# Block-sparse attention with a gated MLP behind it: small tiles gathered in front, large tiles at round SBUF addresses, the sampled words loaded as one plain row

## The chip, the core and the metric

The kernel runs on one core of one Trainium2 chip. Times are device microseconds (us) of one execution. The core has TensorE (PE, with its weight loads shown apart as PEld), VectorE (DVE), ScalarE (ACT), GpSimd (POOL) and SyncE (SP). SP, ACT and POOL issue DMAs; sixteen DMA engines carry them out. SBUF has 128 partitions, and a tile's address below is the byte at which it starts in each of them.

## What is computed

```python
# batch 4, heads 8, sequence 768, head size 64, blocks of 32, 3 sampled blocks per query block
scores = scale * np.matmul(q, k.transpose(0, 1, 3, 2))
...
mask = mask | (blk_i == 0) | (blk_j == 0) | (blk_i == n_blocks - 1) | (blk_j == n_blocks - 1)
for qb in range(n_blocks):
    for kb in sampled_blocks[qb]:
        mask[qb * block:(qb + 1) * block, kb * block:(kb + 1) * block] = True
...
x = attn_out.transpose(0, 2, 1, 3).reshape(B * S, H * D)      # 3072 x 512
h = x @ w_in                                                 # 512 x 2048
g = h * (1.0 / (1.0 + np.exp(-1.702 * h)))
return (g @ w_out).astype(np.float32)                        # 2048 x 512
```

The mask also holds each block's own neighbours. `sampled_blocks` is int64, 24 x 3 values.

## The kernel before

The 3072 tokens are worked in `NC` = 6 chunks of `CT` = 512. Each chunk needs eight units of attention (64 query rows of all heads each), which fill one chunk tile pair `xhi`, `xlo`; there are `NX` = 3 such pairs, `x[0]`, `x[1]`, `x[2]`, used in turn. Every fp32 factor of the MLP is held as a high and a low half in fp32r, and every product is three matmuls: high by high, high by low, low by high.

`first` (line 903) works the attention of the first chunk while inputs still arrive. `tick` (line 694) then runs 64 steps, one for each pair of a chunk (the first four) and one of the 16 slices of 128 hidden columns. A step has `up` (line 548), 12 matmuls in the order L557, L558, L559 with a slice of `win` as weights (the stationary operand) and 512 columns of `xhi` or `xlo` streamed through (the moving operand); the gate on ACT and DVE into `ghi` and `glo`; and `down` (line 588) for the step before, 12 matmuls at L608, L609 and L604 with `ghi` or `glo` as weights and 512 columns of `wout` streamed. Attention of later chunks is put between the steps by `plan`. `last` and `pair` (lines 890 and 835) do the last two chunks together, in seven products of half size for eight: L817 in `half`, with `win`, or sums of them in `shi`, `slo`, as weights and `x` or `t2hi`, `t2lo` streamed. In all there are 768 matmuls at L557 to L559, 1152 at L604 to L609 and 336 at L817, each of 128x128 weights and 512 columns.

`win0` to `win6` and `wout0` to `wout2` lie in the pool `const`; `win7` to `win15` in the pool `late`, which takes the room of the opening tiles once those are done with; `x[2]` in the pool `stage`, behind `late`. `ghi`, `glo`, `g` and `wst` lie in the pool `work`. `prepare` closes the attention pools and opens `tail` at the right end. No address is written in the code: pools are stacked in the order in which they are opened, those of the left from below, those with `side="right"` from the top, so a small tile in one pool shifts all that come behind it.

`run` (line 959) sets the order of the opening. SP issues, in this order: the keys of batch 0 (`kres`, three DMAs at L220), the sampled words for value loads (`sbr`, L140), the same words in all partitions (`scratch`, L153), values (`vown`, L250), queries (`qt`, L206), the keys of batch 1 (L220, two DMAs), and so on. L140 takes the low half of each int64:

```python
        self.sbr = const.tile([1, NB, NR], I32, name="sbr")
        nc.sync.dma_start(out=self.sbr.rearrange("p a b -> p (a b)"), in_=sb32.rearrange("(o a c) -> o a c", o=1, c=2)[:, :, 0])
```

`load_k` (line 210) reads single words of `sbr` into registers, on POOL at L233 and on SP at L243.

Of the kernel before, what the change touches and what calls it, by code (L numbers as in the profile page):

```python
# [9 lines left out]
F32 = mybir.dt.float32  # L10
F32R = mybir.dt.float32r
I32 = mybir.dt.int32
# [6 lines left out]
P = 128  # L19
B, H, S, D = 4, 8, 768, 64  # L20
BLK = 32
NB = S // BLK
NPAIR = H // 2
NR = 3
# [30 lines left out]
class Kernel:  # L55
# [4 lines left out]
    def __init__(self, ctx, tc, q, qd, kb, kT, v, vd, sb, w_in, w_out, out):  # L60
        self.tc, self.nc = tc, tc.nc
        self.q, self.qd, self.kb, self.kT, self.v, self.vd, self.sb = q, qd, kb, kT, v, vd, sb
        self.w64, self.out = (w_in.bitcast(I32), w_out.bitcast(I32)), out
        self.ctx = ctx
        pool = self.pool = lambda name, bufs, **k: ctx.enter_context(tc.tile_pool(name=name, bufs=bufs, **k))
        self.const = pool("const", 1)
        self.work = pool("work", 2)
        self.attnpool, self.wordpool = ExitStack(), ExitStack()
        self.attn = self.attnpool.enter_context(tc.tile_pool(name="attn", bufs=1, side="right"))
        self.words = self.wordpool.enter_context(tc.tile_pool(name="words", bufs=3, side="right"))  # L70
        self.small = pool("small", 6)
        psum = pool("psum", 1, space=PSUM)
        dram = pool("dram", 1, space=DRAM)
        self.ws = [dram.tile([P, DM], F32, name=f"ws{f}") for f in range(NF)]
        self.banks = psum.tile([P, 8, 512], F32, name="banks")
        self.bank = [self.banks[:, i] for i in range(8)]
        c = self.const


        self.kg = [self.attn.tile([P, 12, 2, NPAIR * BLK], F32, name=f"kg{i}") for i in range(RING)]  # L80
        self.qt = [self.attn.tile([P, 2, NPAIR * UT], F32, name=f"qt{i}") for i in range(RING)]
        self.opening = ExitStack()
        early = self.opening.enter_context(tc.tile_pool(name="opening", bufs=1))
        vpool = [self.attn] * RING + [early]
        self.vown = [p.tile([P, 2, 2 * VROW], F32, name=f"vown{i}") for i, p in enumerate(vpool)]
        self.vmid = [p.tile([P, 2 * VROW], F32, name=f"vmid{i}") for i, p in enumerate(vpool)]
        self.win = [c.tile([P, 2 * DM], F32R, name=f"win{f}") for f in range(NWIN)]
        self.wout = [c.tile([P, 2 * DM], F32R, name=f"wout{i}") for i in range(WRING)]
        self.x = [(c.tile([P, NCT, CT], F32R, name=f"xhi{i}"), c.tile([P, NCT, CT], F32R, name=f"xlo{i}"))
                  for i in range(2)]  # L90
        self.kres = early.tile([P, 2, NPAIR, S], F32, name="kres")
        self.raw4 = early.tile([P, 2 * DM], I32, name="raw4")
        self.pts = [self.attn.tile([P, 4, P], F32, name=f"pt{i}") for i in range(3)]
        self.pts += [self.work.tile([P, 4, P], F32, name=f"pt{3 + i}", tag=("ghi", "glo")[i % 2]) for i in range(3)]
        self.npt = 0
        self.kmidof, self.vmidof = [None] * RING, [None] * (RING + 1)
        self.units, self.kent, self.vent, self.items = [], [], [], []

        def entry(of, **more):
            of.append({"n": len(of), "scores": 0, "values": 0, **more})  # L100
            return of[-1]

        def item(k, v, **more):
            k["scores"] += 1
            v["values"] += 1
            self.items.append({"n": len(self.items), "unit": self.units[-1], "k": k, "v": v, **more})

        def dense(b):
            entry(self.units, b=b, u=None)
            k = entry(self.kent, b=b, u=None)  # L110
            for i in range(2):
                v = entry(self.vent, b=b, u=None, i=i)
                item(k, v, i=i, first=i == 0, end=i == 1)

        def sparse(b0, u):
            k, v = (entry(of, b=b0, u=u) for of in (self.kent, self.vent))
            for b in (b0, b0 + 1):
                entry(self.units, b=b, u=u)
                item(k, v, first=True, end=True)

        for b in range(2):
            dense(b)
        sparse(0, 0)
        for b in range(2, B):
            dense(b)
        for n in range(1, 2 * NU):
            sparse(n // NU * 2, n % NU)
        for n, e in enumerate(self.vent):
            e["at"] = n % (RING + 1) if n < NV3 else (n - NV3) % RING
            e["behind"] = next((o for o in reversed(self.vent[:n]) if o["at"] == e["at"]), None)  # L130
        self.knext = self.vnext = 0
        self.early = True
# [3 lines left out]
    def indices(self):  # L136
        nc, const = self.nc, self.const
        sb32 = self.sb.bitcast(I32).rearrange("a b -> (a b)")
        self.sbr = const.tile([1, NB, NR], I32, name="sbr")
        nc.sync.dma_start(out=self.sbr.rearrange("p a b -> p (a b)"), in_=sb32.rearrange("(o a c) -> o a c", o=1, c=2)[:, :, 0])  # L140
        scratch = self.work.tile([P, CT], F32, name="scratch", tag="g")
        at = [0]

        def take(shape):
            n = 1
            for k in shape:
                n *= k
            flat = scratch[:, at[0]:at[0] + n]
            at[0] += n
            return flat.rearrange("p (a b) -> p a b", a=shape[0]) if len(shape) == 2 else flat  # L150
# [16 lines left out]
                           allow_small_or_imprecise_dtypes=True)  # L167
        qb = take([NB])
        nc.gpsimd.iota(qb, pattern=[[1, NB]], base=0, channel_multiplier=0, allow_small_or_imprecise_dtypes=True)
        self.ident = const.tile([P, P], F32, name="ident")  # L170
        make_identity(nc, self.ident)
        yield
        nc.vector.memset(vblk[:, 0:NB:NB - 1], 0.0)
# [18 lines left out]
        for i in range(NR):  # L192
            for cols, rows in ((first, slice(BLK * i, BLK * (i + 1))), (second, slice(BLK * (i + 1), BLK * (i + 2)))):
                nc.vector.tensor_copy(out=vblk[rows, cols], in_=rr[rows, cols, i])
        self.vidx = const.tile([P, 2, NB], I32, name="vidx")
        vrow = take([NB])
        nc.vector.tensor_scalar(out=vrow, in0=vblk, scalar1=float(BLK), scalar2=lane, op0=ALU.mult, op1=ALU.add)
        for b in range(2):
# [87 lines left out]
            pass  # L286

    def psum(self, what, k):  # L290

        early, late = {"s": ((0, 1), (2, 3)), "t": ((4, 5), (4, 5)), "a": ((6,), (7,))}[what], {"s": (0, 1), "t": (0, 1), "a": (2,)}[what]
        return early[k % 2] if self.early else late
# [754 lines left out]
```

## Time and profile before

| | |
|---|---|
| median of 3 runs (lowest to highest) | 753.39 us (751.44 to 754.46) |
| the profiled execution's own time | 752.94 us |
| its span, first to last instruction | 751.2 us |
| PE busy | 726.3 us, 97% of the span |
| DVE, ACT, POOL busy | 450.5, 388.5, 64.9 us |
| chain that ended last | PE 74%, DVE 10%, DMA 9%, ACT 4% |
| DMA | 122.97 MB, mean 164 GB/s |

How to read it: the ends of matmuls are modelled, and a matmul of 512 columns is shown some 395 ns long while the next one starts some 230 ns after it. So "busy" on PE says only that no gap is wider than about 0.16 us, and the pace of PE is read from the starts of successive matmuls, not from their durations.

### The profile page before, as it was taken

The page shows a single profiled execution, that of the slowest core. Times are in us where ns is not written, and L with a number is a line of the kernel's source. Part 1 is how long each engine was busy: PE and PEld are TensorE (multiplying, and loading weights), DVE is VectorE, ACT ScalarE, POOL GpSimd, SP SyncE. Part 2 cuts the span into 40 slices and gives each one's busy share as a digit, 9 for nine tenths or more (in the row PEclk, how much of TensorE's full clock was granted, in tenths as well). Part 3 has the DMA queues.
Part 4 walks back from the last instruction along what each step waited for, and adds up shares of the span by engine and source line. Part 5 has one row for each costly group of instructions (what it writes and reads, how often), then busy time and mean ns, then how long its engine had stood idle before and what let it go on. Part 6 is the DMA issues. An engine that isn't in the chain of part 4 may idle for free.

```text
span 751.2 us, 18756 instructions
## 1 busy us (share of the span) xinstructions
PE 726.3 (97%) x7564; PEld 562.8 (75%) x7564; DVE 450.5 (60%) x839; ACT 388.5 (52%) x759; POOL 64.9 (9%) x105
## 2 busy tenths in 40 slices
PE   7988999998999999999999999999999999999996
PEld 4656777676777777777877777777777788888885
DVE  4676788789654444455444534544576877676542
ACT  4676666666554454445444444544334554545442
POOL 1336201011000110100000000100000000000000
PEclk9999999999999999999999999999999999999999
DMA  8988877768476576657565555630111311110532
GB/s 305 353 319 273 263 263 249 243 213 283 169 230 184 154 207 194 178 159 235 171 186 174 168 167 173 198 98 30 43 43 42 85 28 43 29 42 29 145 107 70
DMA packets 58858, 122.97 MB, mean 164 GB/s; under 512 B 7188, under 2 KB 24980, under 8 KB 58772
## 3 DMA queue, kind: packets, MB, share of 16 engines
q1 hardware_dynamic: 45060, 76.72, 33.8%
q0 software_dynamic: 6336, 23.43, 9.4%
q10 hardware_dynamic: 7376, 21.63, 8.5%
q8 instruction: 59, 0.97, 0.5%
q14 instruction: 27, 0.22, 0.1%
HBM read 111.26 MB, written 10.49 MB: 162 GB/s over the span
## 4 chain that ended last, share of the span: by engine, by line
PE 74%; DVE 10%; DMA 9%; ACT 4%; issue 2%; SPq 1%; ACTq 0%; DVEq 0%
PE banks L604 10%; PE banks L608 10%; PE banks L609 10%; PE banks L817 9%; PE banks L557 6%; PE banks L558 6%; PE banks L559 6%; PE banks L393 5%; PE banks L364 5%; PE banks L315 5%; DMA raw<-in_moe_w_in_dram 2%; DMA vmid<-in_v_dram 2%; DMA raw<-in_moe_w_out_dram 2%; DVE a L509 1%; PE banks L325 1%
## 5 line engine op out<-in xcount | busy, mean ns | idle before, releaser
L609 PE MATMUL banks<-wout,ghi 128*128 128x512 f32 x384 | 152.0, 396 | 1.7 <-DVE wout L477 1.7
L608 PE MATMUL banks<-wout,ghi 128*128 128x512 f32 x384 | 153.2, 399 | 0.0
L604 PE MATMUL banks<-wout,glo 128*128 128x512 f32 x384 | 109.6, 399 | 0.6 <-DVE glo L585 0.6
L346 ACT ACTIVATE ex<-banks,nm 128x256 f32<-128x256 f32 x176 | 69.2, 479 | 77.4 <-DVE rg L409 77.4
L557 PE MATMUL banks<-xhi,win 128*128 128x512 f32 x256 | 105.5, 412 | 1.1 <-DVE g L572 0.8
L559 PE MATMUL banks<-xhi,win 128*128 128x512 f32 x256 | 100.9, 394 | 0.0
L558 PE MATMUL banks<-xlo,win 128*128 128x512 f32 x256 | 100.9, 394 | 0.0
L546 DVE TENSOR_TENSOR wout<-wst,wout 128x512 fp32r<-128x512 f32 x80 | 55.2, 691 | 68.6 <-ACT wout L545 66.2
L609 PEld LDWEIGHTS banks<-wout,ghi 128*128 128x128 f32 x384 | 72.1, 188 | 19.1 <-DVE wout L477 2.5
L608 PEld LDWEIGHTS banks<-wout,ghi 128*128 128x128 f32 x384 | 72.0, 188 | 17.6 <-ACT ghi L577 0.3
L604 PEld LDWEIGHTS banks<-wout,glo 128*128 128x128 f32 x384 | 70.7, 188 | 18.9 <-DVE glo L585 2.2
L565 ACT ACTIVATE g<-banks 128x512 f32<-128x512 f32 x64 | 38.6, 603 | 87.9 <-PE banks L559 87.9
L370 ACT COPY pt<-banks 128x512 f32<-128x512 f32 x112 | 60.9, 589 | 32.4 <-PE banks L364 29.0
L261 POOL DMA_INDIRECT vown<-in_v_dram,vidx x44 | 44.2, 1004 | 381.3 <-PE banks L393 370.1
L577 ACT CAST ghi<-g 128x512 fp32r<-128x512 f32 x80 | 50.1, 626 | 44.2 <-DVE g L572 38.0
L572 DVE SCALAR_TENSOR_TENSOR g<-g,banks 128x512 f32<-128x512 f32 x51 | 35.0, 686 | 60.4 <-ACT g L565 60.1
L332 DVE TENSOR_REDUCE mx<-banks 128x4 f32<-128x1024 f32 x44 | 53.7, 1221 | 25.6 <-PE banks L315 25.6
L364 PEld LDWEIGHTS banks<-ident,ex 128*128 128x128 f32 x448 | 51.0, 141 | 17.3 <-ACT pt L370 6.5
L364 PE MATMUL banks<-ident,ex 128*128 128x128 f32 x448 | 60.7, 276 | 2.5 <-ACT pt L370 2.3
L557 PEld LDWEIGHTS banks<-xhi,win 128*128 128x128 f32 x256 | 48.1, 188 | 13.5 <-ACT wst L570 1.3
L393 PEld LDWEIGHTS banks<-vown,pt 128*32 128x32 f32 x1408 | 42.2, 109 | 19.1 <-issue 14.5
L559 PEld LDWEIGHTS banks<-xhi,win 128*128 128x128 f32 x256 | 48.1, 188 | 11.2
(111 smaller groups left out, 1096.3 us busy)
## 6 DMA issues: line engine op xcount, KB each, us to landing
wst<-ws SPq DMA_DIRECT2D x80, 256.0 KB, 2.7
kg<-in_kb_dram SPq DMA_DIRECT2D x126, 128.0 KB, 3.2
raw<-in_moe_w_in_dram ACTq DMA_DIRECT2D x16, 512.0 KB, 5.6
raw<-in_moe_w_out_dram ACTq DMA_DIRECT2D x16, 512.0 KB, 4.9
kg<-in_kb_dram SPq DMA_DIRECT2D x18, 384.0 KB, 3.8
vown<-in_vd_dram SPq DMA_DIRECT2D x8, 780.0 KB, 11.7
vmid<-in_v_dram SPq DMA_DIRECT2D x22, 260.0 KB, 3.9
qt<-in_q_dram SPq DMA_DIRECT2D x22, 256.0 KB, 3.3
```

Source lines behind the costliest of these rows:

```text
L346: nc.scalar.activation(out=ex[:, cols], in_=sps[h][:, cols], func=AF.Exp, bias=un["nm"][:, c:c + 1], scale=SCALE)
L364: self.nc.tensor.transpose(ps[:, slot], g["ex"][h][:, k * P:(k + 1) * P], self.ident)
L370: self.nc.scalar.copy(out=pt, in_=ps)
L393: nc.tensor.matmul(sums[BLK * c:BLK * (c + 1), 2 * i + h], g["pt"][h][:, 2 * i + k, BLK * c:BLK * (c + 1)], src[:, at:at + DV], start=(k = ...
L546: self.nc.vector.tensor_tensor(out=t[:, DM:2 * DM], in0=w, in1=t[:, 0:DM].bitcast(F32), op=ALU.subtract)
L557: nc.tensor.matmul(h, wih[:, k], hi[:, k], start=(k == 0), stop=False)
L558: nc.tensor.matmul(h, wih[:, k], lo[:, k], start=False, stop=False)
L559: nc.tensor.matmul(h, wil[:, k], hi[:, k], start=False, stop=(k == NCT - 1))
L604: nc.tensor.matmul(o[n], glo[:, tk[n]], woh, start=False, stop=last)
L608: nc.tensor.matmul(o[n], ghi[:, tk[n]], woh, start=(f == 0), stop=False)
L609: nc.tensor.matmul(o[n], ghi[:, tk[n]], wol, start=False, stop=False)
L817: self.nc.tensor.matmul(bank, a[:, k], b[:, k], start=start and k + n == 0, stop=k == 1 and n == 2, skip_group_check=True)
```

## The change

The tiles `sbr`, `ident`, `vidx` and the pool `small` move from the ends of `const` and behind `work` to the front of SBUF, with 192 bytes of filling, and 480 bytes of filling are put at the right end. The DMA of the sampled words takes both halves of every int64 as one row of 144 words, and readers step over the high halves.

```diff
         pool = self.pool = lambda name, bufs, **k: ctx.enter_context(tc.tile_pool(name=name, bufs=bufs, **k))
+        self.bits = pool("bits", 1)
+        self.small = pool("small", 6)
+        self.fill(self.bits, 192)
         self.const = pool("const", 1)
         self.work = pool("work", 2)
+        self.fill(pool("top", 1, side="right"), 480)
         self.attnpool, self.wordpool = ExitStack(), ExitStack()
         self.attn = self.attnpool.enter_context(tc.tile_pool(name="attn", bufs=1, side="right"))
         self.words = self.wordpool.enter_context(tc.tile_pool(name="words", bufs=3, side="right"))
-        self.small = pool("small", 6)
...
-        self.sbr = const.tile([1, NB, NR], I32, name="sbr")
-        nc.sync.dma_start(out=self.sbr.rearrange("p a b -> p (a b)"), in_=sb32.rearrange("(o a c) -> o a c", o=1, c=2)[:, :, 0])
+        words = self.bits.tile([1, NB, NR, 2], I32, name="sbr")
+        nc.sync.dma_start(out=words.rearrange("p a b c -> p (a b c)"), in_=sb32.rearrange("(o n) -> o n", o=1))
+        self.sbr = words[:, :, :, 0]
...
-        self.ident = const.tile([P, P], F32, name="ident")
+        self.ident = self.bits.tile([P, P], F32, name="ident")
...
-        self.vidx = const.tile([P, 2, NB], I32, name="vidx")
+        self.vidx = self.bits.tile([P, 2, NB], I32, name="vidx")
...
+    def fill(self, pool, n):
+        if n:
+            pool.tile([P, n // 4], F32, name="fill")
```

What the pools make of it, as the two programs were laid out. "Remainder" is that of the start address by 64; all slices that matmuls take out of the large tiles start at multiples of 512 bytes inside them.

| tile | start before | remainder | start after | remainder |
|---|---|---|---|---|
| win0 to win6, wout0 to wout2, x[0], x[1] | 8320 + a multiple of 2048 | 0 | 10240 + a multiple of 2048 | 0 |
| ghi, glo, wst, g (work) | 83040 + a multiple of 2048 | 32 | 83968 + a multiple of 2048 | 0 |
| win7 to win15 (late) | 99872 + a multiple of 4096 | 32 | 100352 + a multiple of 4096 | 0 |
| x[2] (stage) | 136736, 144928 | 32 | 137216, 145408 | 0 |
| gs, t2hi, t2lo, shi, slo (tail) | 163808 + a multiple of 2048 | 32 | 163328 + a multiple of 2048 | 0 |
| ident | 82336 | 32 | 9088 | 0 |
| kg, qt, vown0, ex, pt0 to pt2 (attn) | from 162400 up | 32 | from 161920 up | 0 |

After the change all those of the first four lines start at multiples of 2048, and those of `tail` at 1536 past one, a multiple of 512.

On every engine the instructions stand in the same order as before. The one that differs is the fourth of SP's list, which before begins so (`sbr` is the tile of sampled words, `scratch` their copy in all partitions):

```order
1 L220 DMA kres<-in_kT_dram 128x2x384 x2
2 L220 DMA kres<-in_kT_dram 128x1536
3 L140 DMA sbr<-in_sampled_blocks_dram 1x72x1
4 L153 DMA scratch<-in_sampled_blocks_dram 128x144
5 L250 DMA vown_99<-in_vd_dram 128x1560
6 L206 DMA qt_95<-in_qd_dram 128x256
7 L220 DMA kres<-in_kT_dram 128x1536 x2
```

With the change the same stretch of SP reads:

```order
1 L224 DMA kres<-in_kT_dram 128x2x384 x2
2 L224 DMA kres<-in_kT_dram 128x1536
3 L143 DMA sbr<-in_sampled_blocks_dram 1x144
4 L157 DMA scratch<-in_sampled_blocks_dram 128x144
5 L254 DMA vown_107<-in_vd_dram 128x1560
6 L210 DMA qt_103<-in_qd_dram 128x256
7 L224 DMA kres<-in_kT_dram 128x1536 x2
```

Nothing moved; 72 pieces of one word each became one run of 144 words.

## Rows read from the trace of the kernel before

**Rows 1.** The page, part 1: busy time of each engine.
```profile
PE 726.3 (97%) x7564; PEld 562.8 (75%) x7564; DVE 450.5 (60%) x839; ACT 388.5 (52%) x759; POOL 64.9 (9%) x105
```
**Rows 2.** Stretches: us; busy PE, PEld, DVE, ACT, POOL; PE clock; DMA share, GB/s.
```profile
20.00:60.00 40.00, 34.40 (x643) 23.74 (x638) 28.43 (x66) 28.52 (x53) 13.84 (x31) 0.96 0.96 339
60.00:200.00 140.00, 133.08 (x1638) 101.09 (x1642) 110.91 (x213) 90.34 (x183) 20.40 (x25) 1.00 0.74 242
200.00:550.00 350.00, 350.00 (x4339) 273.25 (x4329) 173.76 (x333) 167.21 (x357) 26.26 (x28) 1.00 0.54 163
550.00:752.00 202.00, 193.30 (x827) 154.31 (x825) 128.09 (x201) 93.60 (x156) 0.00 (x0) 0.99 0.22 60
```
**Rows 3.** Timeline of PE (start, us, what), chunk 3, x[0] with win10.
```profile
539.38 0.39 PE L557 MATMUL banks<-xhi,win 128*128 128x512 f32 x1
...
540.78 0.40 PE L608 MATMUL banks<-wout,ghi 128*128 128x512 f32 x1
...
542.41 0.40 PE L609 MATMUL banks<-wout,ghi 128*128 128x512 f32 x1
```
**Rows 4.** Timeline of PE, chunk 3, x[0] with win0, then with win4.
```profile
464.32 0.39 PE L557 MATMUL banks<-xhi,win 128*128 128x512 f32 x1
...
465.69 0.39 PE L608 MATMUL banks<-wout,ghi 128*128 128x512 f32 x1
...
495.25 0.40 PE L557 MATMUL banks<-xhi,win 128*128 128x512 f32 x1
...
496.63 0.39 PE L557 MATMUL banks<-xhi,win 128*128 128x512 f32 x1
```
**Rows 5.** Timeline of PE, chunk 2, x[2] with win3, then with win7.
```profile
358.30 0.40 PE L557 MATMUL banks<-xhi,win 128*128 128x512 f32 x1
...
359.70 0.39 PE L608 MATMUL banks<-wout,ghi 128*128 128x512 f32 x1
...
390.79 0.39 PE L557 MATMUL banks<-xhi,win 128*128 128x512 f32 x1
...
392.15 0.39 PE L608 MATMUL banks<-wout,ghi 128*128 128x512 f32 x1
```
**Rows 6.** Timeline of PE, last chunks, t2hi and t2lo with shi and slo.
```profile
578.47 0.40 PE L817 MATMUL banks<-t2hi,shi 128*128 128x512 f32 x1
578.71 0.40 PE L817 MATMUL banks<-t2lo,shi 128*128 128x512 f32 x1
...
579.87 0.40 PE L817 MATMUL banks<-xhi,shi 128*128 128x512 f32 x1
```
**Rows 7.** Timeline of SP, the opening: start, us, issue.
```profile
2.28 0.94 SPq L140 DMA_DIRECT2D sbr<-in_sampled_blocks_dram  x1
3.26 0.48 SPq L153 DMA_DIRECT2D scratch<-in_sampled_blocks_dram  x1
...
4.80 3.29 SPq L220 DMA_DIRECT2D kres<-in_kT_dram  x2
```
**Rows 8.** Stretches of the opening, columns as in rows 2.
```profile
6.00:7.00 1.00, 0.95 (x13) 0.29 (x9) 0.00 (x0) 0.00 (x0) 0.00 (x0) 1.00 1.00 412
7.00:8.00 1.00, 1.00 (x9) 1.00 (x10) 0.96 (x1) 0.00 (x0) 0.00 (x0) 1.00 0.13 35
8.00:9.00 1.00, 0.52 (x5) 0.33 (x3) 0.97 (x2) 0.72 (x1) 0.00 (x0) 1.00 0.47 111
9.00:10.00 1.00, 0.76 (x2) 0.19 (x2) 0.21 (x3) 0.85 (x2) 0.00 (x0) 1.00 0.78 256
```
**Rows 9.** DMA of the stretch from 6.7 to 8.5 us: packets by size.
```profile
DMA packets 175, 0.19 MB, mean 103 GB/s; under 512 B 95, under 2 KB 150, under 8 KB 175
```
**Rows 10.** The chain of waits, 0 to 60 us: start, us, what.
```profile
20.41 7.75 DMA vown<-in_vd_dram
...
28.17 13.28 DMA vmid<-in_v_dram
```
**Rows 11.** The tile sbr: POOL's loads, ns min/median/max, first and last start.
```profile
L233 POOLq TENSOR_LOAD <-sbr x24: 283/286/496, 17.5 to 70.5; - x24
```

## The prediction

> **What bounds the kernel now.** I read the page first, then stretches, then the starts of single matmuls. PE is busy for 97% of the span [rows 1]. By stretches, PE has no gap from 200 to 550 us, DVE and ACT are at about half there, and the granted clock is 1.00, the 2.4 GHz level [rows 2]. From 550 us to the end PE runs 193.3 of 202 us. So over most of the span the time is the pace of PE, and the pace of matmuls with 512 columns is what a change of addresses could touch. The other bounded place is the opening: from 20 to 60 us the DMA engines are at a share of 0.96 and PE at 34.4 of 40 us [rows 2], and the chain there goes through two DMAs, 7.75 and 13.28 us long, which end at 41.5 us [rows 10].
>
> For the pace I take the starts of successive matmuls. With x[0] and win10, six matmuls take 540.78 - 539.38 = 1.40 us, 233 ns each; the seven steps of L608 and L609 behind them take 542.41 - 540.78 = 1.63, again 233 ns [rows 3]. At 2.4 GHz, 512 columns need 213 ns, so each matmul has some 20 ns beyond its columns. With the same x[0] and win0, six take 1.37 us (228 ns each), with win4 1.38 (230) [rows 4]. With x[2] it is the other way round: win3 takes 1.40 (233), win7 1.36 (227) [rows 5]. Same lines, same shapes, same clock; what differs is where the tiles start. In the table of addresses, x[0] and win0, win4 both have the remainder 0 by 64, x[2] and win7 both 32; the two slow pairings (x[0] with win10, x[2] with win3) mix 0 and 32. I call a pair of moving and stationary operand **even** when the remainders are equal and **odd** when not. Even pairs ran at 227 to 230 ns in these rows whether both remainders are 0 or both 32, odd pairs at 233. One even pairing speaks against it: t2 with shi and slo (both 32) takes 579.87 - 578.47 = 1.40, 233 ns [rows 6].
>
> **The change, term by term.**
>
> *Pairs that turn from odd to even.* All `down` matmuls are odd now (wout 0, ghi and glo 32): 3 x 384 = 1152. Of `up`, in chunks 0, 1 and 3 (x[0], x[1], x[0]) the nine slices win7 to win15 are odd, in chunk 2 (x[2]) the seven slices win0 to win6: (3 x 9 + 7) x 12 = 408. Of the 336 at L817, the 24 products of shi and slo with x (3 per pass, 8 passes, 6 matmuls: 144) are odd, and of those with win 60 more: a11 and a12 with x[2] in passes 0 to 2 (36), a22 with x[0] in passes 4 to 7 (24). That is 204, and 1152 + 408 + 204 = 1764. The change makes every one of them even.
>
> *What each saves.* The rows bound it: nothing, if they behave like t2 with shi [rows 6]; 233.3 - 226.7 = 6.6 ns, if like x[2] with win7 [rows 5]. I take an even pace of 230 ns, the slower of the two x[0] blocks [rows 4], because `down` has a new pairing for which no row stands: 3.3 ns x 1764 = 5.8 us; the ends are 0 and 11.7 us. About 300 of the 1764 lie in chunk 0, before 200 us, where DVE is busy 110.9 of 140 us and PE loses 7 us to waits [rows 2]; a faster PE partly waits more there, so I take off half of their 1.0 us: **5.3 us gained**. From 200 us on nothing takes it back, since DVE and ACT stand at about half [rows 2].
>
> *Matmuls that don't change class.* Transposes against ident, and the attention's matmuls on kg, qt, vown and pt, have tiles with remainder 32 on both sides before and 0 on both after (the slices inside are the same). I cost them at nothing.
>
> *The sampled words.* Before, L140 costs SP 0.94 us where its neighbour costs 0.48 [rows 7], and its 72 pieces travel as packets of one word. They show at 6.7 to 8.5 us: 95 of the 175 packets are under 512 B and 0.19 MB move in 1.8 us [rows 9]. In the three microseconds from 7 the DMA share is 0.13, 0.47 and 0.78, after 1.00 [rows 8], so 0.87 + 0.53 + 0.22 = 1.62 us of all engines' time are lost while SP hangs in the issue of kres, 3.29 us for two [rows 7]. The row of 576 bytes takes most of that hole away; scratch, behind it, keeps its 128 small rows. The first reader comes at 17.5 us [rows 11], so the words themselves are in no hurry: what gains is the traffic behind them. From 20 us on the engines are at 0.96 [rows 2], the chain to 41.5 us is DMA [rows 10], and PE, DVE and ACT follow it. So I take **1.4 us gained** at 41.5 us, kept to the end because nothing afterwards hangs on an absolute time. The ends: 0, if the backlog is made up elsewhere before 41 us, or 3.0, if PE's wait also shortens so far that the half clock behind it (0.96 in that stretch) doesn't come.
>
> The Trainium skill, DMA: Bandwidth & Descriptors, section Rules for kernel authors, says that a strided last dimension becomes one descriptor per element. The packets agree [rows 9].
>
> *Small things at nothing.* The filling issues no instruction. DMAs into tiles at a remainder of 0 instead of 32: where the engines are full they carry 412 GB/s already [rows 8], and what a packet might save is within the 3.0 above. The register loads of sbr (0.29 us each) [rows 11] step over the high words at no price, for they load one word either way.
>
> *Sum.* 752.94 (the profiled execution, span 751.2) - 5.3 - 1.4 = 746.2. The median of the runs is 0.45 above that execution, so the forecast is **746.7**. With the ends it lies between 753.4 - 11.7 - 3.0 = 738.7 and 753.4.
>
> **Rivals.**
>
> 1. *Addresses count for nothing, and the blocks differ for another reason* (neighbouring work, place in the step). Against it: the crossing of rows 3, 4 and 5, in which neither the chunk nor the slice alone decides. For it: t2 with shi [rows 6], and `down`, the largest term, has no even row at all. Then only the opening is left: 753.4 - 1.4 = 752.0, to be called the same. The Trainium skill, SBUF — State Buffer, section Who interferes with whom, says that PE reads through two ports of its own, one for each operand, and never waits on anyone; by it this rival would hold. The trace differs by 3 to 6 ns a matmul.
>
> 2. *Slower: round addresses fall into step.* Before, no matmul reads both operands from multiples of 512. After, nearly all streams start at a multiple of 2048 and every fourth weight slice too; if the reads of weights and of columns then meet in the same place every time, the pace gets worse, not better. The widest step of the blocks shown is 0.24 us, from 578.47 to 578.71 [rows 6]. At 240 ns against 233, 2256 matmuls cost 16 us: 753.4 + 16 - 1.4 = 768. It decides from a very small point: the opening's 1.4 us is 0.6 ns a matmul, so above 234 ns the kernel is slower than before. The slow even pairing [rows 6] speaks for it; the even pairs of rows 4, where the stream starts at 128 beyond a multiple of 2048 and the weights at 128 beyond a multiple of 512, have the same distance to each other as after the change and speak against it.
>
> 3. *More than any row shows.* Every stream before crosses a 2048 boundary, after the change only those of the tail and attention do. If the 20 ns beyond the columns are a price of that, up to 20 x 2256 = 45 us go: 708. For it speaks only that no row excludes it; against it, that even pairs with quite different starts run alike [rows 4, 5].
>
> **How the numbers follow.** A difference of 0.5%, 3.8 us, is about what a measurement of this kernel can tell from none. The forecast's mechanism gets 0.70, rival 1 0.16, rival 2 0.08, rival 3 0.06. Of the forecast's 0.70 I put 0.05 within 0.5%, as its ends reach to nothing gained. So faster is 0.65 + 0.06 = 0.71, the same 0.05 + 0.16 and 0.02 of rival 2 = 0.23, slower 0.06. The range takes the forecast with its ends and rival 1: 738.5 to 752.5; outside stay rival 3 below, rival 2 above, and the last microsecond of rival 1.
>
> **What would show it.** In the timeline of the changed kernel, six `up` matmuls take 1.36 to 1.38 us with x[0] and win10 and with x[2] and win3, and the L608, L609 run 227 to 230 ns a step; the attention's blocks stay as they are. SP's issue of sbr drops to about 0.5 us, the hole from 7 to 9 us goes, and PE's first L393 with vmid, behind the DMA that ends at 41.5 us now, comes some 1.4 us earlier. The forecast is wrong if `down` still steps at 233 (rival 1), at 235 or more (rival 2), or if all blocks step below 225 (rival 3).

## The result and the profile after

The change made the kernel faster: 742.19 us median of 4 runs (740.48 to 745.56), against 752.41 (750.45 to 754.46) of the kernel before beside it, a ratio of 0.9868 [0.9842, 0.9893] (in brackets, here and below, the 95% interval). A second series, of 6 runs, gave 744.35 (742.52 to 747.47), ratio 0.9887 [0.9860, 0.9914]. The forecast was 746.7, 738.5 to 752.5. The profiled execution took 741.64 us, its span is 739.9.

The page of the changed kernel, part 1:

```profile
PE 719.3 (97%) x7564; PEld 564.2 (76%) x7564; DVE 449.8 (61%) x839; ACT 388.4 (52%) x759; POOL 63.3 (9%) x105
```

Its stretches, columns as in [rows 2]:

```profile
20.00:60.00 40.00, 36.69 (x698) 26.54 (x692) 29.87 (x66) 31.92 (x60) 14.96 (x29) 1.00 1.00 351
60.00:200.00 140.00, 134.19 (x1599) 101.80 (x1595) 111.14 (x213) 88.05 (x179) 16.42 (x22) 1.00 0.73 240
200.00:550.00 350.00, 348.95 (x4330) 275.48 (x4329) 176.10 (x333) 168.28 (x358) 26.21 (x28) 1.00 0.54 162
```

PE still has next to no gap from 200 to 550 us, and its busy time fell by 7.0 us [rows 1]. The pace shows it. Chunk 3, x[0] with win10, and `down` behind it, the place of [rows 3] (timeline: start, us, what):

```profile
532.18 0.39 PE L565 MATMUL banks<-xhi,win 128*128 128x512 f32 x1
...
533.54 0.39 PE L616 MATMUL banks<-wout,ghi 128*128 128x512 f32 x1
...
535.12 0.39 PE L617 MATMUL banks<-wout,ghi 128*128 128x512 f32 x1
```

The six take 1.36 us (227 ns each; 233 before), and the seven steps of `down` 1.58 (226; 233 before). x[2] with win3, 1.40 us in [rows 5], and t2 with shi and slo, 1.40 in [rows 6], now read:

```profile
353.08 0.39 PE L565 MATMUL banks<-xhi,win 128*128 128x512 f32 x1
...
354.44 0.39 PE L616 MATMUL banks<-wout,ghi 128*128 128x512 f32 x1
...
571.09 0.39 PE L825 MATMUL banks<-t2hi,shi 128*128 128x512 f32 x1
...
572.45 0.39 PE L825 MATMUL banks<-xhi,shi 128*128 128x512 f32 x1
```

Both take 1.36. The t2 block was even before and is even now, yet it too became faster.

The opening, SP's issues, beside [rows 7]:

```profile
2.30 0.33 SPq L143 DMA_DIRECT2D sbr<-in_sampled_blocks_dram  x1
2.68 0.36 SPq L157 DMA_DIRECT2D scratch<-in_sampled_blocks_dram  x1
...
4.20 0.94 SPq L224 DMA_DIRECT2D kres<-in_kT_dram  x2
```

and its stretches, beside [rows 8]:

```profile
6.00:7.00 1.00, 1.00 (x14) 0.41 (x4) 0.29 (x1) 0.00 (x0) 0.00 (x0) 1.00 0.99 385
7.00:8.00 1.00, 1.00 (x11) 1.00 (x9) 0.97 (x3) 0.05 (x1) 0.00 (x0) 1.00 0.48 38
8.00:9.00 1.00, 0.29 (x3) 0.10 (x3) 0.88 (x3) 0.85 (x2) 0.00 (x0) 1.00 0.78 244
9.00:10.00 1.00, 0.81 (x6) 0.14 (x6) 0.61 (x5) 0.90 (x1) 0.00 (x0) 1.00 1.04 437
```

The issue of `sbr` fell from 0.94 to 0.33 us and that of `kres` from 3.29 to 0.94. The hole of 1.62 us is 0.52 + 0.22 = 0.74 now; what is left goes with the 128 rows of `scratch`, for it is gone where another queue issues them (`scratch_act` below). From 6.7 to 8.5 us 24 packets are under 512 B, 95 before [rows 9]:

```profile
DMA packets 159, 0.19 MB, mean 106 GB/s; under 512 B 24, under 2 KB 139, under 8 KB 159
```

The chain of 0 to 60 us, beside [rows 10]:

```profile
19.88 6.63 DMA vown<-in_vd_dram
26.53 11.95 DMA vmid<-in_v_dram
38.48 0.14 issue
38.61 1.11 PE banks L401 x62
```

The second DMA ends at 38.48 us, 3.0 us before the 41.45 of the kernel before. How much of that is the row, and how much differs from one execution to the next, comes out below.

**Where the time went.** Three points of the program split the span: the first 512-column matmul, the 385th (chunk 0's own 384 are done) and the last. The last two points in the timeline of the kernel before:

```profile
203.13 0.39 PE L608 MATMUL banks<-wout,ghi 128*128 128x512 f32 x1
...
744.48 0.39 PE L604 MATMUL banks<-wout,glo 128*128 128x512 f32 x1
```

and of the changed kernel:

```profile
199.77 0.39 PE L616 MATMUL banks<-wout,ghi 128*128 128x512 f32 x1
...
733.25 0.39 PE L612 MATMUL banks<-wout,glo 128*128 128x512 f32 x1
```

| us | to the first | first to 385th | **385th to last** | rest |
|---|---|---|---|---|
| before | 78.66 | 124.47 | **541.34** | 6.70 |
| after | 75.25 | 124.53 | **533.48** | 6.63 |
| after, second series | 78.02 | 126.38 | **533.38** | 6.64 |

The third column is the pace of 1872 matmuls, and it is steady: in the eight profiled kernels whose pairs are all even it lies between 533.38 and 533.61, and in the two with the addresses of before at 541.34 and 541.33. The change takes **7.9 us** there. Nearly all that is left of the difference between two executions comes out of the first 205 us.

### The profile page after: what moved, and what is told of

Read it like the earlier page. It is cut to its first block, busy times and chain, and to the rows that moved or that the text cites. A ratio compares the mean times of both kernels' runs of the same rounds, so it can differ in the third digit from the quotient of the medians.

```text
span 739.9 us, 18756 instructions
## 1 busy us (share of the span) xinstructions
PE 719.3 (97%) x7564; PEld 564.2 (76%) x7564; DVE 449.8 (61%) x839; ACT 388.4 (52%) x759; POOL 63.3 (9%) x105
## 4 chain that ended last, share of the span: by engine, by line
PE 74%; DVE 11%; DMA 7%; ACT 5%; issue 2%; SPq 1%; ACTq 0%; POOL 0%; DVEq 0%
PE banks L612 10%; PE banks L616 10%; PE banks L617 9%; PE banks L825 9%; PE banks L565 6%; PE banks L566 5%; PE banks L567 5%; PE banks L401 5%; PE banks L372 5%; PE banks L323 5%; DMA raw<-in_moe_w_in_dram 2%; DMA vmid<-in_v_dram 2%; PE banks L333 1%; DVE g L580 1%; DVE a L517 1%
## 5 line engine op out<-in xcount | busy, mean ns | idle before, releaser
L616 PE MATMUL banks<-wout,ghi 128*128 128x512 f32 x384 | 151.5, 395 | 0.0
L617 PE MATMUL banks<-wout,ghi 128*128 128x512 f32 x384 | 149.9, 390 | 1.3 <-DVE wout L485 1.3
L612 PE MATMUL banks<-wout,glo 128*128 128x512 f32 x384 | 107.6, 394 | 1.2 <-DVE glo L593 1.2
L265 POOL DMA_INDIRECT vown<-in_v_dram,vidx x44 | 42.7, 970 | 380.2 <-PE banks L401 367.9
```

The source lines that it names most:

```text
L612: nc.tensor.matmul(o[n], glo[:, tk[n]], woh, start=False, stop=last)
L616: nc.tensor.matmul(o[n], ghi[:, tk[n]], woh, start=(f == 0), stop=False)
L617: nc.tensor.matmul(o[n], ghi[:, tk[n]], wol, start=False, stop=False)
```

## The experiments

In the table, a matmul's *distance* is the start of its moving operand less that of its stationary one, as the remainder by 256 (why 256 comes out below). Counted the shorter way round, 160, 176, 192, 224 and 240 are 96, 80, 64, 32 and 16; the text names them so. The columns go by the weights: those of L817 that have `win` as weights stand with `up`. The pace is the mean step from the start of one 512-column matmul to that of the next in the profiled execution, in ns; steps over 260 ns are left out. "Stretch" is the 385th to the last, in us.

| kernel | `ghi`, `glo` as weights (`down`): distance, pace | `win` as weights (`up` and part of L817): distance, pace | `shi`, `slo` as weights (rest of L817): distance, pace | stretch |
|---|---|---|---|---|
| before | 32: 233.2 | 0: 230.2; 96: 233.1; 160: 233.7 | 0: 232.3; 160: 233.2 | 541.34 |
| after | 0: 227.6 | 0: 228.5 | 0: 227.0 | 533.48 |
| all32 | 0: 227.5 | 0: 228.5 | 0: 226.8 | 533.41 |
| wout32 | 160: 233.6; 224: 233.5 | 0: 229.1; 128: 232.3 | 0: 228.4 | 540.44 |
| work64 | 192: 233.1 | 0: 230.2; 128: 232.4 | 0: 232.1; 128: 232.6 | 541.41 |
| glo16 | 0: 228.8; 176: 231.8; 240: 228.6 | 0: 229.3; 128: 232.5 | 0: 228.2; 128: 232.3 | 537.08 |
| g256 | 0: 227.5 | 0: 228.4 | 0: 226.9 | 533.54 |
| g32 | 224: 232.7 | 0: 229.6 | 0: 227.7 | 538.87 |

### One part at a time

`row_only`: the plain row alone. Its tile lies in a pool at the right end; this moves the buffers of raw weight words, `raw` and `a`, by 576 bytes and leaves every tile that matmuls read where it was.

```diff
+        self.row = self.attnpool.enter_context(tc.tile_pool(name="row", bufs=1, side="right"))
...
-        self.sbr = const.tile([1, NB, NR], I32, name="sbr")
...
+        const.tile([1, NB, NR], I32, name="room")
+        words = self.row.tile([1, NB, NR, 2], I32, name="sbr")
...
```

> The plain row alone, every large tile at its address of before. If the opening and the pace of PE are two separate gains, only the opening changes: SP's issue of the sampled words falls from 0.94 to about 0.33 us, the first matmul of the first step comes about 3 us earlier than in the kernel before (78.7 us there, 75.3 us in the changed kernel), down still steps at 233 ns, and the time is 749 to 750.5 us. If the earlier opening comes from the new addresses instead (DMA into them, or PE), the time stays at 752.4 us.

752.19 us (12 runs), 0.9988 [0.9970, 1.0006]: no gain clear of the scatter; the interval reaches from 2.3 us faster to 0.5 us slower. The profiled execution reached the first 512-column matmul at 75.89 us, 2.77 before the kernel before, and the 385th at 203.67, 0.54 behind it. It lost its lead in chunk 0, where its chain reads:

```profile
135.65 6.12 DMA raw<-in_moe_w_out_dram
...
141.85 5.66 DMA raw<-in_moe_w_in_dram
```

PE's work of chunk 0 hangs on weight slices that are fetched, split and used one after the other; from 135.65 to 147.51 the chain is two fetches. In the kernel before, fetches of 5.25 us from 128.20 and of 4.44 us from 142.95 stand in the chain, and the second ends at 147.39: this execution's lead was gone by then.

`addr_only`: the addresses of the change, the 72 pieces of before.

```diff
-        self.fill(self.bits, 192)
+        self.fill(self.bits, 480)
...
-        words = self.bits.tile([1, NB, NR, 2], I32, name="sbr")
-        nc.sync.dma_start(out=words.rearrange("p a b c -> p (a b c)"), in_=sb32.rearrange("(o n) -> o n", o=1))
-        self.sbr = words[:, :, :, 0]
+        self.sbr = self.bits.tile([1, NB, NR], I32, name="sbr")
+        nc.sync.dma_start(out=self.sbr.rearrange("p a b -> p (a b)"), in_=sb32.rearrange("(o a c) -> o a c", o=1, c=2)[:, :, 0])
```

> The new addresses alone, the sampled words loaded in 72 pieces as before. If the gains are separate: down and up step at 227 to 229 ns as in the changed kernel, the opening is that of the kernel before (first matmul of the first step at about 78.5 us), and the time is 744.5 to 746 us. If the addresses also made the opening shorter, about 742 us.

745.31 us (6 runs), 0.9895 [0.9868, 0.9922]; the stretch 533.50. The addresses are nearly the whole gain. Whether the row adds anything when all pairs are even was asked again, with both kernels side by side:

> The changed kernel once more, beside the next one on the same chip: what the plain row of sampled words is worth when all pairs are even. Theory (most of the opening's gain is given back in chunk 0's weight chain): at most 1.5 us faster than the next, 742 to 744.5 us. Rival (the opening's gain of 1.3 to 1.4 us is kept, and more by the half clock that does not come): 1.5 to 3.5 us faster, 741 to 743 us.

> The changed kernel with the 72 pieces of one word back in place of the plain row, addresses as in the changed kernel. Theory: at most 1.5 us slower than the one before it, 743 to 745.5 us. Rival: 1.5 to 3.5 us slower, 744.5 to 746 us. The stretch from the 385th to the last 512-column matmul is 533.5 us in both by either.

744.35 us with the row and 744.22 with the pieces (6 runs each), 0.9887 [0.9860, 0.9914] and 0.9883 [0.9859, 0.9906]: no difference that can be told. The medians speak against the rival, 1.5 to 3.5 us kept; but each interval is some 2 us wide to either side, so a gain of 1 or 2 us is not excluded. The chain of the kernel with the row has the two fetches again at the same place:

```profile
137.67 5.83 DMA raw<-in_moe_w_out_dram
...
143.57 4.56 DMA raw<-in_moe_w_in_dram
```

and that of the kernel with the pieces:

```profile
136.25 6.14 DMA raw<-in_moe_w_out_dram
...
142.47 6.32 DMA raw<-in_moe_w_in_dram
```

They end at 148.13 and 148.79, near the 147.51 of `row_only` and the 147.39 of the kernel before; but of these four only `row_only` had a lead, the two new ones reach their first 512-column matmul at 78.02 and 77.78. In the changed kernel's first profile the same fetch, 4.47 us from 139.21, ends at 143.68, and all of the 3.4 us of lead is still there at the 385th matmul.

All fourteen profiles side by side say more than these chains. The wait is the one near 40 us, which a DMA of `vmid` or `vown` ends in the chain; in the second series with the row that is

```profile
27.27 12.68 DMA vmid<-in_v_dram
```

and so 39.95 us. The clock is the granted one from 40 to 50 us. `scratch_act` is left out of the table, because its keys come late.

| profiled kernels | wait ends, us | clock | first 512-column matmul, us | 385th, us |
|---|---|---|---|---|
| with the row: `after`, `row_only`, `wout32`, `work64`, `glo16`, `g256`, `raw_ahead` (its chain does not show the wait) | 38.48 to 39.83 | 1.00 | 75.05 to 76.13 | 198.96 to 203.83 |
| with the row: `after_again`, `all32`, `g32` | 39.95 to 40.24 | 0.83 | 78.02 to 79.44 | 204.40 to 206.73 |
| with the pieces: `addr_only`, `addr_again` | 39.96, 41.58 | 1.00 | 76.59, 77.78 | 203.11, 205.17 |
| with the pieces: before | 41.45 | 0.83 | 78.66 | 203.13 |

With the row the wait ends at 39.4 us on the mean of nine, with the pieces at 41.0 on the mean of three: 1.6 us, with a scatter of the same size. From there to the first 512-column matmul it is 36.2 to 36.8 us where the clock is 1.00 and 37.2 to 39.5 where it is 0.83, and the lower clock comes with the row and without it. A lead is not given back as a rule: the seven of the first line are 2.7 us ahead of the other seven profiles at the first 512-column matmul, on the mean, and 3.0 us at the 385th. `row_only` is the exception; why its weights came late stays open.

### Round starts or equal starts

`all32`: all tiles 32 bytes further up, so that no stream starts at a multiple of 2048, and all pairs are even.

```diff
-        self.fill(self.bits, 192)
+        self.fill(self.bits, 224)
...
-        self.fill(pool("top", 1, side="right"), 480)
+        self.fill(pool("top", 1, side="right"), 448)
```

> All tiles of the changed kernel 32 bytes further up, so that every pair stays even but nothing starts at a multiple of 64, let alone of 2048. If only the distance between the two operands counts (even pairs), the pace stays at 227 to 229 ns and the time at 742 us. If round starts count, or streams that cross no 2048 boundary, the pace goes back to 230 to 233 ns and the time to 748 to 752 us.

744.78 us (4 runs), 0.9875 [0.9841, 0.9909], the stretch 533.41. Crossing a multiple of 2048 costs nothing that the stretch shows; rival 3 falls, and the round addresses are no part of the gain.

`wout32`: `wout` meant to be the one odd tile.

```diff
-        self.fill(self.bits, 192)
+        self.fill(self.bits, 64)
...
-        self.wout = [c.tile([P, 2 * DM], F32R, name=f"wout{i}") for i in range(WRING)]
+        self.wout = [c.tile([P, 2 * DM + 8], F32R, name=f"wout{i}")[:, o:o + 2 * DM] for i, o in enumerate((8, 0, 8))]
+        self.fill(c, 32)
```

> Only wout0 to wout2 start at a remainder of 32, all other tiles at 0, so the 1152 matmuls of down are odd and all others even. If odd pairs cost what the rows of before show, down steps at 233 ns and up stays at 227 to 229, and the time rises by 1152 x 5 to 6 ns, 6 us, to about 748 us. If addresses count through something else than the pair (DVE and ACT writing into the tiles, the opening), down stays at 227 and the time at 742 us.

750.57 us (10 runs), 0.9981 [0.9956, 1.0005]. Nearly everything is lost again, more than `down` alone should cost: `up` got slower too. I first laid that to the neighbourhood of odd matmuls. The table shows the other half of the reason: the smaller filling had put win0 to win6 128 bytes from all the `x` tiles, and these pairs step at 232.3. A distance of 128 is not even.

### How far apart is apart

`work64`: all remainders by 64 stay 0, but `work` starts 64 bytes further on.

```diff
-        self.fill(self.bits, 192)
+        self.fill(self.bits, 64)
         self.const = pool("const", 1)
+        self.fill(pool("step", 1), 64)
         self.work = pool("work", 2)
+        self.fill(pool("next", 1), 64)
```

> All large tiles keep the remainder 0 by 64, but the work pool (ghi, glo) now starts 64 bytes past a multiple of 128 against wout, and win7 to win15 and x[2] are shifted by other odd or even counts of 64 against x[0], x[1] and win0 to win6. Theory (what counts is whether the starts of the two operands agree by 64, nothing larger): the pace stays at 227 to 229 ns in every block, ratio to the kernel before 0.985 to 0.991, 741.5 to 746 us. Rival (the unit is 128 bytes or more): down steps at 233 ns, as in the kernel with wout alone shifted by 32, and the time is 749 to 753 us.

751.49 us (10 runs), 0.9986 [0.9964, 1.0009]. My theory fell: a distance of 64 is as slow as one of 32. Chunk 3, x[0] with win10 (distance 128), and `down` (192):

```profile
537.44 0.39 PE L567 MATMUL banks<-xhi,win 128*128 128x512 f32 x1
...
538.83 0.39 PE L618 MATMUL banks<-wout,ghi 128*128 128x512 f32 x1
...
540.46 0.40 PE L619 MATMUL banks<-wout,ghi 128*128 128x512 f32 x1
```

1.39 us for six, 1.63 for seven steps: 232 and 233 ns.

`glo16`: `glo` 16 bytes off; its tiles grow by 64 bytes.

```diff
-        self.fill(self.bits, 192)
+        self.fill(self.bits, 64)
...
-        glo = self.work.tile([P, CT], F32R, name="glo")
+        glo = self.work.tile([P, CT + 16], F32R, name="glo")[:, 4:CT + 4]
```

> Only glo lies 16 bytes past a multiple of 64; all else has the remainder 0. The 384 matmuls with glo as weights are the only odd ones. Theory (any difference by 64 makes a pair slow, and neighbours of slow pairs are slowed by about half as much): wout with glo at 233 ns, wout with ghi and up about 229 to 230, in all 384 x 5.5 + 768 x 2 = 3 to 4 us over the changed kernel: 745 to 747 us, ratio 0.989 to 0.993. Rival (only a difference of 32 or more counts): as the changed kernel, 741 to 744 us, ratio 0.984 to 0.989. Rival (a start that is not a multiple of 32 is worse than one of 32): wout with glo above 236 ns and over 748 us.

746.86 us (8 runs), 0.9921 [0.9896, 0.9945]. As in `wout32` the filling made 128s besides, so the total says little, but the two buffers of `glo` came to lie at distances of 16 and 80 (240 and 176 in the table): with 16 `down` steps at 228.6, as its even neighbours with `ghi` at 228.8, with 80 at 231.8. So 16 bytes cost nothing that can be seen here.

`g256` and `g32`: all tiles at one remainder, `work` alone 256 bytes away from it, or 32.

```diff
-        self.fill(self.bits, 192)
+        self.fill(self.bits, 0)
...
+        self.fill(pool("step", 1), 256)
         self.work = pool("work", 2)
-        self.fill(pool("top", 1, side="right"), 480)
+        self.fill(pool("next", 1), 256)
+        self.fill(pool("top", 1, side="right"), 160)
```

(32 and 480 for the two fillings around `work` in `g32`.)

> All large tiles at one remainder by 512, but the work pool (ghi, glo) 256 bytes away from it: the down matmuls alone have their two operands 256 apart by 512, up and the last chunks' products stay equal. Stretch from the 385th to the last 512-column matmul, 533.5 us in the changed kernel. Theory (what counts is the distance by 512 or more; distances of 128 and 384 cost 4 to 5 ns a matmul): down at 232 to 233 ns, its even neighbours at 229 to 230, the stretch 538.5 to 540.5 us. Rival (the unit is 256): down at 227 to 228 ns and the stretch 533 to 534 us. Rival (256 apart is the worst case): down above 235 ns, the stretch above 542 us.

> The same with the work pool 32 bytes away in place of 256: the down matmuls alone are odd, by 32 as in the kernel before; up and the last chunks' products stay equal. Theory (even matmuls that stand next to odd ones are slowed too, so that most of the gain comes from down): down at 233 ns, up at 229.5 to 230.5 and the stretch from the 385th to the last 512-column matmul 539.5 to 541 us, nearly all of the 541.3 of the kernel before. Rival (every matmul by its own pair, no neighbours): up at 227 to 228, the stretch 533.5 + 960 x 5.6 ns = 538.9 us or less.

`g256`: 742.83 us (2 runs), 0.9866 [0.9827, 0.9905], the stretch 533.54. The rival holds: 256 apart is as good as 0. The same place of chunk 3:

```profile
531.58 0.39 PE L567 MATMUL banks<-xhi,win 128*128 128x512 f32 x1
...
532.93 0.39 PE L618 MATMUL banks<-wout,ghi 128*128 128x512 f32 x1
...
534.52 0.39 PE L619 MATMUL banks<-wout,ghi 128*128 128x512 f32 x1
```

and in `g32`:

```profile
541.86 0.39 PE L567 MATMUL banks<-xhi,win 128*128 128x512 f32 x1
...
543.23 0.39 PE L618 MATMUL banks<-wout,ghi 128*128 128x512 f32 x1
...
544.85 0.40 PE L619 MATMUL banks<-wout,ghi 128*128 128x512 f32 x1
```

Seven steps of `down` take 1.59 us with 256 (227 ns) and 1.62 with 32 (231 in this block, 232.7 on the mean). `g32` took 750.40 us (8 runs), 0.9963 [0.9942, 0.9984], its stretch 538.87: 5.3 us more than `g256`, which is what `down` alone is worth there. The even matmuls with `win` as weights step at 228.4 in `g256` and 229.6 in `g32`: odd neighbours cost an even one about 1 ns, and the rival (no neighbours, 538.9 or less) is nearer than my theory (539.5 to 541).

### Can the first 205 us be had

`raw_ahead` fetches each weight slice of chunk 0 one further ahead, into a fourth buffer (the lines that make that buffer and free it are left out here).

```diff
-            for n in range(asked[0], min(k + 1 + self.early, len(todo))):
-                scalar(lambda n=n, own=self.early and n % 4 == 3: go(n, own))
+            ahead = self.early or self.extra is not None
+            for n in range(asked[0], min(k + 1 + ahead, len(todo))):
+                scalar(lambda n=n, own=ahead and n % 4 == 3: go(n, own))
...
```

> The changed kernel with a fourth buffer for raw weight words once the opening tiles are closed, so that in chunk 0 each slice is fetched one further ahead. Theory (chunk 0 is held by the wait for raw words: that chain took the gain of the opening and of the pace there): chunk 0 ends 2 to 5 us earlier than in the changed kernel and so does the whole: 737 to 740 us, ratio 0.979 to 0.984. Rival (chunk 0 is held by DVE's and ACT's conversion or by the DMA engines' total, not by how early a fetch is asked for): 741 to 744 us, ratio 0.984 to 0.989. Rival (earlier weight fetches delay attention's inputs): 744 to 747 us.

742.10 us (4 runs), 0.9861 [0.9823, 0.9899]: not to be told from the changed kernel. The waits for `raw` are gone from the chain, and others stand in their place, the way of the split halves to DRAM and back:

```profile
136.63 6.93 DMA ws<-a
...
155.67 4.86 DMA ws<-a
...
173.37 4.00 DMA wst<-ws
```

First to 385th took 123.54 us, 124.53 in the changed kernel's profile and 126.38 in that of its second series. If the fetch ahead gains anything, it is about 1 us against the changed kernel's first profile, within the scatter. No version here beats the changed kernel.

`scratch_act` issues `scratch` on ACT's queue in place of SP's.

```diff
-        nc.sync.dma_start(out=sb_i.rearrange("p a b c -> p (a b c)"), in_=sb32.partition_broadcast(P))
+        nc.scalar.dma_start(out=sb_i.rearrange("p a b c -> p (a b c)"), in_=sb32.partition_broadcast(P))
```

> The changed kernel with the copy of the sampled words in all partitions (128 rows of 576 bytes) issued by ACT in place of SP. In the changed kernel the DMA share still falls to 0.48 in the microsecond from 7. Theory (what the opening gains is mostly given back in chunk 0): the hole from 7 to 9 us gets smaller by up to 0.7 us and the end moves by less than 0.5 us: 741.5 to 743 us, ratio 0.985 to 0.988. Rival (the opening's gain is kept to the end): 740.5 to 741.5. Rival (ACT's queue is in its way): slower by up to 2 us, 744.

748.39 us (8 runs), 0.9939 [0.9915, 0.9963], slower than all I expected; the profiled execution, 744.13 us, is the fastest of the eight and shows only part of it. The hole is gone, in the stretch from 7 us:

```profile
7.00:8.00 1.00, 0.15 (x4) 0.15 (x8) 0.00 (x0) 0.00 (x0) 0.00 (x0) 1.00 1.03 429
```

and yet the chain reaches the first scores later:

```profile
1.27 6.53 DMA kres<-in_kT_dram
7.80 0.04 issue
7.85 0.95 PE banks L333 x8
```

In the changed kernel the chain has L333 at 4.85 us. The DMA engines are full (a share of 1.03), and the first keys take 6.53 us; that they wait behind the rows of `scratch` is my reading, which no run takes apart. The first 512-column matmul came 3.11 us later. Its stretch is 533.41 like that of the others, so this execution's loss lies in the first 205 us.

## Why the prediction was right, and where it was not

- **The bound: right.** From 200 us on the time is the pace of PE, and addresses set it: `g32` differs from `g256` by 224 bytes in the place of one pool, and by 5.3 us in the stretch. The Trainium skill, SBUF — State Buffer, section Who interferes with whom, has PE read through ports of its own and never wait on another engine; if so, what holds up the odd pairs lies within PE's own two reads, of which that page says nothing; no run here tests that.
- **Even and odd: the right pairs, by the wrong unit.** I sorted by 64. The unit is 256: distances of 32, 64, 80, 96 and 128 are slow, 0 and 256 fast (`work64`, `glo16`, `g256`). In the kernel before both sortings name the same matmuls, so the 1764 stood.
- **3.3 ns a matmul: the term that was mis-sized.** The price is 233.2 - 227.6 = 5.6 for `down`. I took 230 as the even pace from [rows 4], and those blocks stood between odd ones. Matmul by matmul, where both traces have the step after the 385th: 902 of `down` gave 5.05 us, 331 with `win` as weights that turned even 1.79, 143 with `shi` or `slo` 0.89, and 357 that had been even all along 0.71. Less 0.6 lost in the other 138 steps this is the 7.9 us of the stretch; my 3.3 ns on its 1764 - 300 = 1464 odd ones make 4.8. The t2 block [rows 6], which I held against the rule, was even, and its pace goes with its neighbours: 232.3 (before) and 232.1 (`work64`) where `down` and the other products of `shi` and `slo` are odd, 227.8 to 229.7 where some of these are even (`g32`, `glo16`, `wout32`), 227.1 to 227.5 where all pairs are.
- **Chunk 0 at half: not settled.** First to 385th took 124.47 us before and 124.53 after. Step by step, 345 of its 384 steps gave 1.40 us there and the other 39, where attention and waits lie between, took 1.46 back. But the steps over 260 ns add up to anything from 44.2 to 48.2 us in the fourteen profiles, and the whole to 123.5 to 127.8, odd or even; a term of 0.5 us cannot be read there.
- **The opening, 1.4 us "kept to the end because nothing afterwards hangs on an absolute time": its size fits, its worth at the end is not settled.** At the end of the wait the profiles give 1.6 us on the mean, from only three with the pieces; the 3.0 of the first profile are more by the luck of two executions. That a lead is kept, they bear out on the mean, though fetches of weights lie between. But whole runs cannot tell the row from nothing: 0.7 us between the medians in `row_only`, and 0.1 the other way in the second series, with intervals that hold both 0 and 1.4. The rule of the Trainium skill, DMA: Bandwidth & Descriptors, section Rules for kernel authors, that a strided last dimension becomes one descriptor per element, agrees with the packets (95 small ones, then 24).
- **The half clock.** The kernel before had a granted clock of 0.96 from 20 to 60 us, the changed one 1.00 [rows 2]. In the second series it was there again with the row, from 40 to 50 us 0.83 in the mean, and not with the pieces; in all it shows in three of ten profiles with the row and in one of three with the pieces (`scratch_act`, 1.00, aside). So it is not the row that decides, as the upper end of the term, 3.0, had it:

```profile
40.00:50.00 10.00, 9.90 (x180) 6.30 (x181) 7.37 (x17) 6.45 (x12) 4.53 (x11) 0.83 0.87 338
```

- **The sum.** 5.3 + 1.4 = 6.7 was forecast. The runs bear out 7.9 for the addresses, and for the row something between nothing and some 2 us; 752.4 - 7.9 = 744.5 is the second series. The first series' 742.19 lies 2 us lower. Its profile has 3.4 us of lead at the 385th matmul, where the profile of the second series is 1.3 behind: scatter of the first 205 us and not of the change.
- **The rivals.** Rival 1 fell with the stretch of `addr_only`, rival 2 with `down` at 227.6, rival 3 with `all32` and with no pace in the table below 226.8.

## What to carry to other kernels

Where PE streams fp32r matmuls of 512 columns back to back, give all large tiles that meet in a matmul the same start by 256, and put small tiles in a pool of their own in front, where they can't shift the others; the roundness of the address itself is worth nothing. Judge such a change by the stretch between two fixed matmuls in the part where PE never waits: it repeats to 0.2 us, while whole runs scatter by 5. And a gain of a microsecond in a part that scatters by several is not to be read from one profile: set all profiles side by side first, with the clock of each.

## What the runs showed of the hardware

- The pace of 128x512 fp32r matmuls depends on where the two operands lie to each other: 227 to 229 ns at a distance of 0 or 256 bytes where all pairs are even, 232 to 234 at 32, 64, 80, 96 and 128. Even pairs among odd ones lie between (228 to 232). At 16 it was 228.6, beside even ones at 228.8. What 48 does, and what in the chip makes it so, no run here shows.
- The even pace takes some matmuls to settle. In the changed kernel, behind attention's small matmuls, the second and third with `win` as weights in an unbroken series step at 233 on the mean (50 of each) and the eighth and later at 227.0 (507 of them); among odd neighbours an even one does not come down to that. This is read from starts; no run took it apart.
- Nearly all scatter between executions that the profiles show lies in the first 205 us; from there to the last matmul eight profiled kernels agree to 0.23 us. Part of it goes with the granted clock, which was 0.83 from 40 to 50 us, behind the wait near 40 us, in four of the fourteen profiles and 1.00 in ten: the way to the first 512-column matmul was then 0.4 to 3.3 us longer.
